# One scaled copy of k moved behind two evictions on VectorE, and a warm-up loop six units shorter

## The chip, the cores and the metric

The kernel runs on one core of a Trainium2 chip. The metric is device time in microseconds (us): the median of three runs of the kernel before is 266.46 us (265.84 to 266.88). The profile is of a single execution of the same program. TensorE (PE), VectorE (DVE), ScalarE (ACT) and GpSimd (POOL) do the work; SyncE (SP) issues most of the transfers.

## The reference

```
q, k, v: (8, 12, 448, 64);  x = attention output, heads side by side: (8, 448, 768)
q_n = q / sqrt(mean(q*q, -1) + 1e-6) * g_q          # the same for k with g_k
attn = softmax(q_n @ k_n.T / sqrt(64));  x = attn @ v
h = relu(x @ w_in);  u, w = h[..., :512], h[..., 512:]      # w_in: 768 x 1024
w_n = (w - mean(w, -1)) / sqrt(var(w, -1) + 1e-6)
gated = u * (w_spatial @ w_n + b_spatial)            # w_spatial: 448 x 448, over the sequence
out = gated @ w_out                                  # 512 x 768, float32
```

## The kernel before

The attention part works in 24 groups. Group G is four heads of one batch (three groups make a batch), so group 15 is the first of batch 5. The steps of a group are short functions named by one letter:

- L loads q or k (second number 0 for q, 1 for k) to a tile `raw`; Q squares it to `sqt`; R sums the squares on DVE (`ss`); I and J turn the sums of q and k to `rs` by Ln and Exp on ACT; N multiplies `raw` by `rs` to the bf16 tile `nrm`, mostly on POOL.
- T is a transposing DMA, issued by SP, from `nrm` to `qT`, or for k to `kr`. Z then multiplies `kr` by a column of gains (`g_col`) to `kT`; it is the scaled copy of the title. Groups 0 to 3 go by matmul transposes (p, P) and copies (k, K) instead.
- S makes scores on PE into two PSUM banks, in 7 units (c = 0 to 6) of a group; E takes the exponential of such a pair on ACT (`et`). s, a and b are the passes over `et` that give the sums of the softmax and the two halves of attention times v; D and d on ACT make the reciprocal sums, X on DVE writes the normalised result to `xt`.

The other part works on one batch at a time, a few steps behind: V and U are the two halves of x times `w_in`; c and u are their ReLU evictions from PSUM; B, M, m and A are the normalisation of the c half; H is the product with `w_spatial`, G the gate, O the product with `w_out`, o its eviction to `os`, t the store. v loads v, and W does the rows left over (384 to 447) of V and O.

The order of all of it is written out by hand: a long string `PLAN` has one word for every step. `S.15.0/23` is step S of group 15, unit 0, into banks 2 and 3; a last part `/v`, `/a` or `/g` names the engine (VectorE, ScalarE, GpSimd). Each engine executes its own words strictly in this order and waits, by semaphores, for what a step reads or overwrites. Because buffers are few (2 tiles `kr`, 4 `kT`, 3 `sqt`, 8 PSUM banks), a late step also holds up whoever writes its buffer next.

One more rule ties DVE and POOL. Steps of either that go through `port` (Q, N, Z from `kr`, A) take turns, so that each waits for the last such step that the other engine has ahead of it in the plan:

```
def port(eng, inst):
    other = on_port.get("g" if eng is dve else "v")
    if other is not None:
        sync_dep(inst, other)
    on_port["v" if eng is dve else "g"] = inst
```

`z.72.18/0` is a warm-up loop on PE in front of the first real matmuls. Its results are not used. The first number counts units of 128 columns, the second says how many matmuls are 512 columns wide (four units each); the rest are 128 wide, so 72.18 is 18 wide matmuls and 66.16 is 16 wide and 2 narrow ones (L269 in the profile). The steps right behind it are the first transposes of group 0 (p.0.0, L469), which read `nrm` from n.0.0 on DVE (L450).

Lines of the profile that come up below: L302 step L, L391 Q, L403 R, L418 and L425 I and J, L442 N, L497 T, L480 Z on DVE, L523 S, L532 E, L558 the passes s, a and b, L577 and L581 D and d, L587 X, L596 c and u on DVE, L603 V, L677 U, L713 O, L372 and L370 o on DVE and on ACT, L323 v.

Of the kernel before, what the change touches and what calls it, by code (L numbers as in the profile page):

```python
# [18 lines left out]

PLAN = """  # L20
setup//v l.1.0/0 l.0.0/1 l.0.1 g.1//a g.0//a l.1.1 L.1.1/2 q.0.0/0/v r.0.0//v L.1.0/3 L.2.1/4 q.1.0/1/g r.1.0//v wb//g
L.2.0/5 i.0//a j.0//a n.0.0//v z.72.18/0 p.0.0/0 q.1.1//a ws//g gA//v q.0.1//a k.0.0/0/a L.3.1/6 gB/7 n.1.0//v p.1.0/6
r.0.1//v L.5.0/7 r.1.1//v L.3.0/8 v.0.2//g i.1//a j.1//a Q.1.1/2/g gC//v k.1.0/0/v z.16.4/1 S.0.1/67 Q.1.0/1/a
S.0.2/01/f n.1.1//v p.1.1/2 L.4.1/0 n.0.1//v p.0.1/3 R.1.1/0/v wo.0//g k.0.1//v E.0.2/0/a R.1.0//v L.4.0/1 k.1.1//a
Q.2.1/0/g R.2.1/1/v z.16.4/4 S.0.5/23/f S.0.4/01 Q.2.0/2/g E.0.1/1/a I.1.0/0/a v.0.1//g J.1.0/0/a S.0.6/45 E.0.6/2/a
# [62 lines left out]
X.10.1//v V.3.2.1/1 v.4.2//g S.13.4/45 G.2.0//v T.15.1/0 E.13.1/a/a Q.19.0/0/a S.13.3/23 E.13.4/g/a E.13.3/3/a  # L88
G.2.1//v W.3/076 S.13.5/45/f t.0.0 S.14.4/23/f V.3.2.2 L.18.0/3 R.16.1//v I.16.0/0/a c.3.3//v O.2.1.0/0 Q.18.1/1/g
V.3.2.0 J.16.0/0/a N.16.0/2/g o.2.3.1/2/v o.2.3.0//v S.13.6/67 o.2.1.0/3/v E.14.4/8/a E.13.5/0/a c.3.2//a B.3.3//v  # L90
S.13.2/23 t.2.3 E.13.6/i/a v.4.0//g Z.15/1/v S.14.1/45 E.14.1/9/a U.3.3.0/0 v.4.1//g U.3.3.2 U.3.3.1 u.3.3//v
O.2.1.1/7 o.2.1.1//v S.13.0/45 s.12.5.1/01 R.18.1/1/v s.12.6.1 E.13.2/5/a E.13.0/d/a s.12.4.1 N.16.1/3/g T.16.1/0
B.3.2//v S.15.0/23 S.14.6/67 E.15.0/6/a R.17.0/2/v s.12.1.1 s.12.2.1 E.14.6/c/a S.15.2/45 s.12.0.1 s.12.3.1 D.12/1/a
D.13/0/a Q.17.1/1/g R.17.1//v T.16.0/0 V.3.0.0/3 V.3.1.2/2 V.3.1.1 V.3.0.1 R.19.0/0/v E.15.2/b/a L.19.1/2 O.2.2.0/1
V.3.0.2 c.3.0//v O.2.0.0/0 I.17.0/0/a V.3.1.0 c.3.1//v Q.18.0/2/g R.18.0//v B.3.1//v J.17.0/0/a N.17.0/1/g b.12.6.1/76
# [687 lines left out]
```

## Time and profile before

| | |
|---|---|
| runs, median (lowest to highest) | 266.46 us (265.84 to 266.88) |
| the profiled execution | 268.54 us |
| its span, first to last instruction | 266.7 us |
| busy: PE, DVE, ACT, POOL | 254.9, 213.3, 216.8, 127.5 us |
| instructions | 9428 |
| granted TensorE clock, mean | 0.985 |

The span is 1.8 us shorter than the time of the same execution; that rest lies around the instructions. The profiled execution took 2.1 us longer than the median of the runs without a profile, so a sum over its rows is made against 268.54 us. An engine's busy time alone says little here, since four engines hand work to each other all the time; what counts is which wait ends last at a given place. In the rows of a timeline, the first number is the start in us from the first instruction, the second how long the row lasted; rows of equal instructions are merged ("x24"), and a bracket tells of idle time ahead of the row and of what ended it. Ends and starts of neighbours on one engine overlap by a few hundredths, because instructions are pipelined.

### The profile page before, as it was taken

To read this page: it belongs to the slowest core of one execution; us is meant where nothing else is said; L and a number is where in the kernel's file an instruction comes from. 1 tells how busy PE (TensorE), PEld (TensorE's weight loads), DVE (VectorE), ACT (ScalarE), POOL (GpSimd) and SP (SyncE) were. 2 spreads that over 40 slices of the span, in tenths; PEclk is the share of its full clock that TensorE was granted. 3 is DMA by queue.
4 is the path that set the end of the run, shared out by engine and by line. 5 is a ranking of instruction groups with operands and counts; after the bars stand their busy time and mean duration, and the time that the engine had idled before them with its cause. 6 is when DMAs were issued, how large, how long until landed. Compare 5 with 4: busy or idle time off the path is not lost.

```text
span 266.7 us, 9428 instructions
## 1 busy us (share of the span) xinstructions
PE 254.9 (96%) x4025; PEld 129.4 (49%) x4041; DVE 213.3 (80%) x368; ACT 216.8 (81%) x357; POOL 127.5 (48%) x109
## 2 busy tenths in 40 slices
PE   7989999999999999999999999999999999999993
PEld 2454435434545456454455454454455555455561
DVE  4899799998698999979799988898983564476861
ACT  1788999999999999997899999997989983332522
POOL 3686246778874789267888577518210000000000
PEclk9995999999999999999999999999999999999999
DMA  6999997999999999999999999999952051031136
GB/s 194 328 306 312 225 258 98 161 232 222 147 233 288 226 240 187 329 204 186 238 240 223 211 248 182 180 196 264 228 115 118 2 209 32 2 124 57 29 158 227
DMA packets 62690, 51.08 MB, mean 192 GB/s; under 512 B 39160, under 2 KB 58808, under 8 KB 62648
## 3 DMA queue, kind: packets, MB, share of 16 engines
q1 hardware_dynamic: 54304, 42.02, 63.4%
q0 software_dynamic: 8192, 8.27, 20.2%
q8 instruction: 31, 0.51, 0.8%
q10 hardware_dynamic: 152, 0.20, 0.2%
q14 instruction: 11, 0.09, 0.1%
HBM read 38.55 MB, written 11.01 MB: 186 GB/s over the span
## 4 chain that ended last, share of the span: by engine, by line
PE 66%; DMA 11%; DVE 8%; ACT 7%; POOL 4%; issue 3%; SPq 0%; POOLq 0%; DVEq 0%
PE ps L558 13%; PE ps L677 11%; PE ps L523 10%; PE ps L713 10%; PE ps L603 9%; PE ps L691 7%; ACT et L532 5%; DMA raw<-in_q_dram 5%; PE ps L637 3%; DMA qT<-nrm 3%; DMA kr<-nrm 3%; POOL nrm L442 3%; DVE xt L587 1%; DVE ss L403 1%; POOL sqt L391 1%
## 5 line engine op out<-in xcount | busy, mean ns | idle before, releaser
L532 ACT ACTIVATE et<-ps 128x896 bf16<-128x896 f32 x168 | 145.3, 923 | 8.1 <-PE ps L523 7.3
L442 POOL TENSOR_TENSOR nrm<-raw,rs 128x896 bf16<-128x896 f32 x32 | 53.7, 1690 | 23.8 <-ACT rs L425 7.3
L391 POOL TENSOR_TENSOR sqt<-raw 128x896 f32<-128x896 f32 (+1 forms) x28 | 46.1, 1650 | 35.4 <-DVE sqt L391 20.1
L523 PE MATMUL ps<-qT,kT 64*32 64x448 bf16 (+1 forms) x1060 | 59.2, 361 | 2.7 <-DMA qT<-nrm 0.6
L403 DVE TENSOR_REDUCE ss<-sqt 128x14 f32<-128x896 f32 x46 | 49.0, 1077 | 1.2 <-POOL sqt L391 1.0
L558 PE MATMUL ps<-et,vt 64*32 64x448 bf16 x1344 | 44.8, 350 | 0.0
L677 PE MATMUL ps<-xt,w_in 128*128 128x448 bf16 x192 | 43.8, 353 | 0.1
L523 PEld LDWEIGHTS <-kT 64*32 64x32 bf16 (+1 forms) x1060 | 21.6, 94 | 33.6 <-issue 21.6
L713 PE MATMUL ps<-w_out,gt 128*128 128x384 bf16 (+1 forms) x196 | 37.5, 323 | 0.1
L603 PE MATMUL ps<-w_in,xt 128*128 128x512 bf16 x128 | 35.6, 380 | 1.0 <-issue 0.3
L587 DVE TENSOR_TENSOR xt<-ps,rc 128x448 bf16<-128x448 f32 x48 | 27.6, 615 | 7.8 <-PE ps L558 6.5
L370 ACT ACTIVATE os<-ps 128x384 f32<-128x384 f32 (+3 forms) x34 | 15.8, 477 | 16.1 <-PE ps L713 12.3
L558 PEld LDWEIGHTS <-vt 64*32 64x32 bf16 x1344 | 22.3, 92 | 12.0 <-issue 3.5
L691 PE MATMUL ps<-w_spT,vn 128*128 128x448 bf16 (+1 forms) x128 | 27.7, 353 | 0.1
L677 PEld LDWEIGHTS <-w_in 128*128 128x128 bf16 x192 | 17.5, 98 | 19.8 <-issue 5.3
L323 POOL DMA_DIRECT2D vt<-in_v_dram x36 | 24.0, 668 | 6.5 <-PE ps L523 6.5
L558 PE MATMUL ps<-et,ones 64*32 64x448 bf16 x672 | 25.9, 353 | 0.4 <-ACT et L532 0.4
L713 PEld LDWEIGHTS <-gt 128*128 128x128 bf16 x196 | 18.3, 98 | 16.0 <-issue 2.8
L372 DVE COPY os<-ps 128x384 f32<-128x384 f32 (+3 forms) x33 | 17.3, 535 | 10.7 <-PE ps L713 6.7
L696 DVE TENSOR_TENSOR gt<-ps,us 128x448 bf16<-128x448 f32 x32 | 19.5, 622 | 6.9 <-PE ps L691 6.1
L652 DVE BATCH_NORM_STATS2 s<-vs 128x6 f32<-128x512 bf16 (+1 forms) x32 | 21.8, 682 | 1.6 <-ACT vs L594 1.4
L603 PEld LDWEIGHTS <-xt 128*128 128x128 bf16 x144 | 12.7, 97 | 16.7 <-issue 5.4
(61 smaller groups left out, 255.8 us busy)
## 6 DMA issues: line engine op xcount, KB each, us to landing
raw<-in_k_dram SPq DMA_DIRECT2D x23, 448.0 KB, 6.1
raw<-in_q_dram SPq DMA_DIRECT2D x23, 448.0 KB, 5.7
out_dram<-os SPq DMA_DIRECT2D x23, 384.0 KB, 3.1
vt<-in_v_dram POOLq DMA_DIRECT2D x24, 112.0 KB, 5.8
vt<-in_v_dram POOLq DMA_DIRECT2D x12, 224.0 KB, 7.4
out_dram<-os SPq DMA_DIRECT2D x9, 192.0 KB, 4.3
w_in<-in_moe_w_in_dram POOLq DMA_DIRECT2D x1, 1536.0 KB, 14.1
w_out<-in_moe_w_out_dram POOLq DMA_DIRECT2D x4, 192.0 KB, 4.5
```

The lines of the kernel that those rows point to most:

```text
L323: pool.dma_start(out=vts[b % 2][64 * halves[0]:64 * halves[0] + 64 * len(halves), g].rearrange("p r c d -> p r (c d)"), in_=src)
L391: port(eng, eng.tensor_tensor(out=t, in0=x, in1=x, op=ALU.mult))
L403: dve.tensor_reduce(out=sss[where["ssl", pair[G]]][:, G - pair[G], i].rearrange("p r c -> p (r c)"), in_=sqt[where.pop(("sq", G, i))].rear ...
L442: port(eng, eng.tensor_tensor(out=nrm[sl[0]].rearrange("p c r d -> p r c d"), in0=raw[where["raw", G, i]].rearrange("p r (c d) -> p r c d" ...
L523: pe.matmul(out=ps[at:at + w, sl[n], 0:S], lhsT=kT[64 * r:64 * r + 64, c, 64 * hh + x:64 * hh + x + w], rhs=qT[64 * r:64 * r + 64, :, 64 * ...
L532: act.activation(out=ets[sl[0]].rearrange("k n (p c) -> k n p c", c=C), in_=ps[:, a:a + 2, 0:S].rearrange("k n (c p) -> k n p c", p=T), fu ...
L558: pe.matmul(out=ps[32 * l:32 * l + 32, where[kind, G][0], 0:S], lhsT=w, rhs=et_of(G, r, c)[at:at + 64], start=(n == 1), stop=(n == C), til ...
L587: dve.tensor_tensor(out=xts[b % 2][:, 2 * g + half, :], in0=ps[:, where.pop(("ab"[half], G))[0], 0:S], in1=rcs[where["rc", G]], op=ALU.mult)
L603: pe.matmul(out=ps[:, bank, :], lhsT=xts[b % 2][:, j, 128 * m:128 * m + 128], rhs=w_in[:, j // 2, j % 2, DH:], start=(n == 1 and j == 2 * ...
L677: pe.matmul(out=ps[:, bank, 0:S], lhsT=w_in[:, j // 2, j % 2, 128 * f:128 * f + 128], rhs=xts[b % 2][:, j, :], start=(n == 1 and j == 2 * ...
L691: pe.matmul(out=ps[:, sl[0], 0:S], lhsT=vns[b % SLOTS["vn"]][rows, m, 128 * f:128 * f + 128], rhs=w_spT[rows, m, :], start=(m == 0), stop= ...
L713: pe.matmul(out=ps[:, sl[0], 0:n], lhsT=gts[b % 2][:, f, 128 * m:128 * m + 128], rhs=w_out[:, f, x:x + n], start=(f == 0), stop=(f == 3))
```

## The change

Z.15 (the scaled copy of k of group 15, on DVE) moves down in the plan, behind u.3.3 and o.2.1.1, which are two evictions of PSUM on the same engine. Seen by the other engines it also moves behind S.14.1, E.14.1, the U.3.3 and O.2.1.1 matmuls and the DMA v.4.1, but these sit on other engines and keep their places there. The warm-up loop loses two wide matmuls and gains two narrow ones.

```
-... n.0.0//v z.72.18/0 p.0.0/0 ...
+... n.0.0//v z.66.16/0 p.0.0/0 ...
-S.13.2/23 t.2.3 E.13.6/i/a v.4.0//g Z.15/1/v S.14.1/45 E.14.1/9/a U.3.3.0/0 v.4.1//g U.3.3.2 U.3.3.1 u.3.3//v
-O.2.1.1/7 o.2.1.1//v S.13.0/45 s.12.5.1/01 R.18.1/1/v ...
+S.13.2/23 t.2.3 E.13.6/i/a v.4.0//g S.14.1/45 E.14.1/9/a U.3.3.0/0 v.4.1//g U.3.3.2 U.3.3.1 u.3.3//v
+O.2.1.1/7 o.2.1.1//v Z.15/1/v S.13.0/45 s.12.5.1/01 R.18.1/1/v ...
```

On VectorE, at 133.85 us of the profile before, the order of instructions changes as follows. L652 and L653 are B.3.3, L480 is Z.15 (reading the tile `kr` and writing the second `kT`), L596 is u.3.3, L372 is o.2.1.1 and L403 is R.18.1.

```order
 L652 BN_STATS s61_151<-vs1_132 64x6 [waits DVE_49]
 L653 BN_AGGR mv1_145<-s61_151 64x2 [waits DVE_49]
+L596 TENSOR_SCALAR us1_136<-ps_63 128x448 [waits PE_49]
+L372 COPY os3_142<-ps_63 128x384 [waits PE_49,Activation_49]
 L480 TENSOR_SCALAR kT1_87<-kr0_84,g2_col_162 128x896 [waits DMAHW6_49,Pool_49]
-L596 TENSOR_SCALAR us1_136<-ps_63 128x448 [waits PE_49]
-L372 COPY os3_142<-ps_63 128x384 [waits PE_49,Activation_49]
 L403 TENSOR_REDUCE ss1_114<-sqt1_74 128x14
 L652 BN_STATS s60_150<-vs1_132 128x6
```

The copy's own waits stay the same: the landing of a DMA (T.15.1) and POOL (its turn behind N.16.0).

On TensorE the order of instructions stays the same. What changes is a wait, at the first weight load of S.15.0 (135.48 us of the profile before), behind the last pass of s.12.4 (L558):

```order
 L558 LDWEIGHTS ones_159
 L558 MATMUL ps_63<-et16_106,ones_159 32x448
-L523 LDWEIGHTS kT1_87 [waits DMAHW5_49]
+L523 LDWEIGHTS kT1_87 [waits DMAHW5_49,DVE_49]
 L523 MATMUL ps_63<-qT3_83,kT1_87 32x448 [waits Activation_49]
 L523 LDWEIGHTS kT1_87
```

The load now waits for DVE itself. Before, the wait of the first pass of s.12.5, a few rows ahead, covered it: that pass writes bank 0, which u.3.3 empties, and u.3.3 stood behind Z.15.

At the start of the program, on TensorE, the end of the warm-up loop changes; the L469 rows are p.0.0:

```order
 L269 MATMUL ps_63<-ident_156 128x512
 L269 LDWEIGHTS ident_156
-L269 MATMUL ps_63<-ident_156 128x512
+L269 MATMUL ps_63<-ident_156 128x128
 L269 LDWEIGHTS ident_156
-L269 MATMUL ps_63<-ident_156 128x512
+L269 MATMUL ps_63<-ident_156 128x128
 L469 LDWEIGHTS nrm00_125 [waits DVE_49]
 L469 MATMUL ps_63<-ident_156,nrm00_125 64x128
```

The instructions of ScalarE, GpSimd and SyncE stand in the same order with the same waits.

More of the change, by code (lines that the diff above doesn't have):

```diff
@@ L21 @@
 setup//v l.1.0/0 l.0.0/1 l.0.1 g.1//a g.0//a l.1.1 L.1.1/2 q.0.0/0/v r.0.0//v L.1.0/3 L.2.1/4 q.1.0/1/g r.1.0//v wb//g
-L.2.0/5 i.0//a j.0//a n.0.0//v z.72.18/0 p.0.0/0 q.1.1//a ws//g gA//v q.0.1//a k.0.0/0/a L.3.1/6 gB/7 n.1.0//v p.1.0/6
+L.2.0/5 i.0//a j.0//a n.0.0//v z.66.16/0 p.0.0/0 q.1.1//a ws//g gA//v q.0.1//a k.0.0/0/a L.3.1/6 gB/7 n.1.0//v p.1.0/6
 r.0.1//v L.5.0/7 r.1.1//v L.3.0/8 v.0.2//g i.1//a j.1//a Q.1.1/2/g gC//v k.1.0/0/v z.16.4/1 S.0.1/67 Q.1.0/1/a
@@ L90 @@
 V.3.2.0 J.16.0/0/a N.16.0/2/g o.2.3.1/2/v o.2.3.0//v S.13.6/67 o.2.1.0/3/v E.14.4/8/a E.13.5/0/a c.3.2//a B.3.3//v
-S.13.2/23 t.2.3 E.13.6/i/a v.4.0//g Z.15/1/v S.14.1/45 E.14.1/9/a U.3.3.0/0 v.4.1//g U.3.3.2 U.3.3.1 u.3.3//v
-O.2.1.1/7 o.2.1.1//v S.13.0/45 s.12.5.1/01 R.18.1/1/v s.12.6.1 E.13.2/5/a E.13.0/d/a s.12.4.1 N.16.1/3/g T.16.1/0
+S.13.2/23 t.2.3 E.13.6/i/a v.4.0//g S.14.1/45 E.14.1/9/a U.3.3.0/0 v.4.1//g U.3.3.2 U.3.3.1 u.3.3//v
+O.2.1.1/7 o.2.1.1//v Z.15/1/v S.13.0/45 s.12.5.1/01 R.18.1/1/v s.12.6.1 E.13.2/5/a E.13.0/d/a s.12.4.1 N.16.1/3/g T.16.1/0
 B.3.2//v S.15.0/23 S.14.6/67 E.15.0/6/a R.17.0/2/v s.12.1.1 s.12.2.1 E.14.6/c/a S.15.2/45 s.12.0.1 s.12.3.1 D.12/1/a
```

## The prediction

> **What bounds the kernel now.** I read the page's busy times and its chain first, then the chain of waits around and behind the moved copy, then the timelines of the four engines around 134 us, and last the start. From the page:
>
> ```profile
> PE 254.9 (96%) x4025; PEld 129.4 (49%) x4041; DVE 213.3 (80%) x368; ACT 216.8 (81%) x357; POOL 127.5 (48%) x109
> PE 66%; DMA 11%; DVE 8%; ACT 7%; POOL 4%; issue 3%; SPq 0%; POOLq 0%; DVEq 0%
> ```
>
> PE has work for 96% of the span and holds two thirds of the chain that ended last. Whether PE also has slack at the place of the change is told by the busy times of stretches (length, then busy time of PE, weight loads, DVE, ACT and POOL):
>
> ```profile
> 135.00:137.00 2.00, 2.00 (x88) 1.22 (x84) 1.92 (x3) 2.00 (x4) 1.48 (x2) 1.00 1.22 253
> 141.00:143.00 2.00, 2.00 (x81) 1.37 (x88) 1.93 (x4) 2.00 (x5) 2.00 (x2) 1.00 0.92 311
> 168.00:266.00 98.00, 93.57 (x1338) 49.34 (x1343) 65.74 (x126) 63.25 (x108) 13.18 (x13) 1.00 0.51 129
> ```
>
> From 135 to 143 us all four are nearly full: nobody has a gap in which to hide a delay. From 168 us PE stays near full while DVE and ACT have a third of their time free. In the chain of waits from 155 us to the end PE is left only once for long:
>
> ```profile
> 159.94 0.02 DVEq L587
> 160.00 2.23 DVE xt L587 x4
> ```
>
> These are X.14 and X.15, which wait for PE's own passes by way of ACT. So what PE loses at 135 to 145 us is not regained by a wait that would have come anyway; it moves the end.
>
> **The moved copy, before.** DVE around it:
>
> ```profile
> 133.18 0.17 DVE L653 BATCH_NORM_AGGREGATE mv<-s 64x2 f32<-64x6 f32 x1
> 133.85 0.62 DVE L480 TENSOR_SCALAR kT<-kr,g_col 128x896 bf16<-128x896 bf16 x1 [0.49 <-DMA kr<-nrm]
> 134.39 0.61 DVE L596 TENSOR_SCALAR us<-ps 128x448 bf16<-128x448 f32 x1
> 135.08 0.56 DVE L372 COPY os<-ps 128x384 f32<-128x384 f32 x1
> 135.55 1.07 DVE L403 TENSOR_REDUCE ss<-sqt 128x14 f32<-128x896 f32 x1
> ```
>
> DVE stands idle for 0.49 us until the transposed k has landed, copies, and goes on with the two evictions. The question is whether these were kept waiting by the copy. Their inputs on PE:
>
> ```profile
> 133.01 1.31 PE L677 MATMUL ps<-xt,w_in 128*128 128x448 bf16 x6
> 134.16 0.81 PE L713 MATMUL ps<-w_out,gt 128*128 128x384 bf16 x4
> 135.10 0.75 PE L558 MATMUL ps<-et,ones 64*32 64x448 bf16 x24
> 135.67 0.56 PE L523 MATMUL ps<-qT,kT 64*32 64x448 bf16 x16
> ```
>
> The matmuls of u.3.3 (L677) end at 133.01 + 1.31 = 134.32, and it began at 134.39. Those of o.2.1.1 (L713) end at 134.16 + 0.81 = 134.97, and it began at 135.08. Both began as soon as PE had delivered, so taking the copy out of their way gains nothing here; the idle time of DVE only moves from the front of the copy to the front of the evictions.
>
> **What the move costs, step by step.** (1) On DVE the copy takes the place at 135.55. Its usual length is in the view of the tile `kr`:
>
> ```profile
> L480 DVE TENSOR_SCALAR kT<-kr,g_col x16: 435/446/621, 52.1 to 195.3; 128x896 bf16<-128x896 bf16 x16
> DMA to landing us min/median/max: 2.9/4.6/8.3
> ```
>
> Its 0.62 us is the longest of 16; I take the median of 0.45, since POOL, which was issuing transfers of v until 134.25 (below), will be idle. It ends at 136.00. The sentence of a page on this: the Trainium skill, "SBUF — State Buffer", on the two physically separate sides, says that VectorE and GpSimd share a pair of ports which the one that starts first holds for its whole instruction, and that descriptors of GpSimd's transfers need it too. By that rule the long copy is such a meeting and 0.45 holds; without it the copy would keep 0.62 and the sum below would be 0.17 us larger.
>
> (2) PE's S.15.0 reads this copy. It began at 135.67 (first of the L523 x16); with the copy done at 136.00 and some 0.1 us to the first matmul it begins at about 136.1: 0.45 us later, and PE executes in order.
>
> (3) POOL takes turns with DVE, so N.16.1 waits for the copy:
>
> ```profile
> 132.88 1.37 POOL L323 DMA_DIRECT2D vt<-in_v_dram  x2
> 134.56 1.69 POOL L442 TENSOR_TENSOR nrm<-raw,rs 128x896 bf16<-128x896 f32 x1 [0.30 <-DVE kT L480]
> 136.76 3.42 POOL L391 TENSOR_TENSOR sqt<-raw 128x896 f32<-128x896 f32 x2 [0.52 <-POOL nrm L442]
> 140.37 3.34 POOL L442 TENSOR_TENSOR nrm<-raw,rs 128x896 bf16<-128x896 f32 x2 [0.19 <-ACT rs L425]
> ```
>
> It began 0.09 us after the copy's end (134.47), so now at 136.09, which is 1.53 us later, and ends at 137.78. Behind it is Q.17.1. Before, that step did not follow at once: it waits for R.18.1, which reads the same `sqt` (135.55 + 1.07 = 136.62, then 136.76). This wait takes up part: Q.17.1 now begins at about 137.74 (neighbours overlap 0.04), 0.98 us later.
>
> (4) From here everything is tight. R.17.1 on DVE reads Q.17.1, and ACT's I.17.0 reads R.17.1:
>
> ```profile
> 138.48 1.09 DVE L403 TENSOR_REDUCE ss<-sqt 128x14 f32<-128x896 f32 x1
> 140.47 0.68 DVE L596 TENSOR_SCALAR vs<-ps 128x512 bf16<-128x512 f32 x1
> 139.66 0.32 ACT L418 ACTIVATE ls<-ss,eps 128x28 f32<-128x28 f32 x1
> 141.04 0.48 ACT L370 ACTIVATE os<-ps 128x384 f32<-128x384 f32 x1
> 143.75 0.46 DVE L480 TENSOR_SCALAR kT<-kr,g_col 128x896 bf16<-128x896 bf16 x1
> ```
>
> Q.17.1 ended at 136.76 + 1.68 (half of 3.42, with the overlap) = 138.44, and R.17.1 began at 138.48; I.17.0 began 0.09 us after R.17.1's end. So c.3.0 (140.47), I.17.0, o.2.0.0 (141.04), N.17.0 (140.37, on `rs`), N.17.1, and Z.16 (143.75, which waits its turn behind N.17.1's end at 143.71) all move by 0.98 us. PE needs three of them at once:
>
> ```profile
> 141.31 0.37 PE L523 MATMUL ps<-qT,kT 64*32 64x448 bf16 x8
> 141.50 0.37 PE L558 MATMUL ps<-et,vt 64*32 64x448 bf16 x8
> 144.45 0.38 PE L523 MATMUL ps<-qT,kT 64*32 64x448 bf16 x8
> ```
>
> S.14.0 (141.31) writes bank 3, emptied by c.3.0 0.15 us earlier; the pass at 141.50 writes bank 0, emptied by o.2.0.0 at 141.52; S.16.1 (144.45) reads Z.16's copy, done at 144.21. With these 0.98 us later PE is 0.98 us late at 142 us and still at 145. That includes the 0.45 us of step (2); the two don't add.
>
> (5) The queues behind: SP issues T.16.1 when N.16.1 is done, 1.53 us later, and T.16.0, L.19.1 and L.20.1 stand behind it.
>
> ```profile
> 136.27 1.26 SPq L497 DMA_TRANSPOSE kr<-nrm  x1
> 125.83 3.19 SPq L497 DMA_TRANSPOSE kr<-nrm  x1
> ```
>
> T.16.1 then goes out at 137.80 and has until Z.16 at 144.73, which is 6.9 us; the median landing takes 4.6. I cost it at nothing; the cover is gone at a landing over 6.9 us (a rival below).
>
> **The warm-up loop.**
>
> ```profile
> 1.69 6.27 PE L269 MATMUL ps<-ident 128*128 128x512 bf16 x18 [1.69 <-POOL ident masks.py:199]
> 8.13 0.58 PE L469 MATMUL ps<-ident,nrm 128*64 128x128 bf16 x7 [0.17 <-DVE nrm L450]
> 4.52 10.33 DMA raw<-in_q_dram
> 19.77 0.88 PE ps L461 x7
> ```
>
> The loop ends at 7.96, and the transposes behind it wait for DVE until 8.13 anyway. Two wide matmuls fewer end it some 0.3 us earlier (1.69 + 6.27 over 18 rows is 0.35 us each; the last ones, at full clock, fewer), and the transposes don't move: zero. If the loop ran late, the first transposes would gain at most 2 x 0.35 = 0.7 us, but the chain there is a transfer of q until 14.85 and reaches PE at 19.77; a gain ahead of it is hidden. A loss is only possible by the clock, below.
>
> **The sum.** +0.98 us from the move, 0 from the loop: 268.54 + 0.98 = 269.5 for an execution with a profile, and the same step on the median of the runs, 266.46 + 0.98 = 267.4. Bounds: 0.45 if only step (2) reaches PE; 1.53 if all of N.16.1's delay does. I take 0.98 because three separate waits of PE have the same value.
>
> **Rivals.** *Absorbed.* Runs without a profile are 2.1 us shorter; if their DVE and POOL have some tenths of slack behind 136 us, only step (2) is left, or a part of it: 266.46 + 0.2 = 266.7. For it: POOL's busy share is 48%. Against it: the rows at 138.48, 141.50 and 143.75 start within 0.1 us of what they wait for.
>
> *Faster.* If the transposed k usually lands later than in this profile, the copy used to hold u.3.3, and with it bank 0 and the passes at 135.10, which now run on. Before, Q.17.1 begins 2.91 us after the copy's start (136.76 - 133.85); now at 137.74 whatever the landing, up to 135.55. They are equal when the copy starts at 134.83, so from a landing 1.0 us later than here the move gains, one for one; at 2 us later the time is 266.46 - 1.0 = 265.4. Against it: this landing took 8.0 us (133.85 - 125.83) already, of a longest 8.3.
>
> *T.16.1 lands late.* At 8.3 us after 137.80 Z.16 begins at 146.1, 2.35 us later than before: 268.8. It decides from 6.9 us. The transposes of this stage show 8.0 and 8.3, but the DMA queues are emptier at 137 than at 126.
>
> *The clock.* The stretches around the fall of the granted clock (ahead of DMA's share):
>
> ```profile
> 6.20:9.62 3.42, 3.25 (x25) 1.83 (x24) 2.79 (x6) 2.33 (x5) 1.97 (x3) 1.00 0.99 324
> 9.62:13.03 3.41, 2.95 (x30) 1.29 (x28) 2.77 (x6) 2.51 (x6) 2.65 (x3) 1.00 1.11 330
> 16.45:19.86 3.41, 2.33 (x53) 1.75 (x50) 3.11 (x5) 2.76 (x6) 3.39 (x5) 1.00 1.09 324
> 19.86:26.69 6.83, 6.75 (x79) 3.47 (x82) 6.28 (x10) 5.76 (x8) 4.39 (x4) 0.50 1.14 314
> ```
>
> The clock fell to half at 19.86, behind the stretch in which PE was busy for 2.33 of 3.41 us. The shorter loop takes some 0.3 us from the first of these, which leaves 2.95, as much as the second had, and no fall came after that one. If it fell there, PE would work at half speed from 9.6 us on, so that the 2.95 us of the second stretch would take twice as long; the chain is on a transfer until 14.85, which covers some of it, so the loss is 0 to 3 us, and at the middle the time is 268.0. The Trainium skill, "TensorE: Matmul & The Clock Gate", part 1, has the rule: an idle window of about 3.4 us halves the clock, a busy one restores it, and the window runs freely, so that its borders differ from run to run. The trace agrees with the halving, and the slow stretch lasts 6.83 us, two such windows; no run here shows what the borders do.
>
> **Chances.** The delay is carried as in the sum: 0.58 (266.9 to 268.0 by its bounds). Absorbed: 0.16. Faster by a later landing: 0.12. T.16.1 late: 0.08. The clock: 0.06. A measurement of this kernel tells about 0.5% from no change, so the limits are 265.13 and 267.79. Slower than that: 0.12 of the first case (its upper end), 0.07 of T.16.1 and the clock's 0.06, together 0.25. Faster: 0.08, of the later landing. The rest, 0.67, is no change that can be told. The range 265.9 to 268.4 leaves out about half of the later landing and of T.16.1, most of the clock's, and some of the first case's edge: under 2 in 10.
>
> **What would show it.** In the profile after: u.3.3 within 0.1 us of its matmuls' end as now; the copy about 1.7 us later against the PE rows around it and 0.45 us long; POOL idle ahead of N.16.1 for some 1.8 us with the copy as its end; DVE idle for about 0.6 us ahead of R.17.1; PE idle some 0.4 us ahead of S.15.0 and again around S.14.0; behind 146 us no new wait. It is wrong if DVE waited long for the landing in ordinary runs, if PE's rows behind 145 us are not late by about 1 us, or if the first 30 us differ.

## The result, and the profile after

The changed kernel took 268.62 us (median of four runs, 268.6 to 268.97), the kernel before 266.57 us (median of four runs, 265.84 to 266.88; three of the four are the runs from which the prediction started): a ratio of 1.0084, 95% interval 1.0062 to 1.0106. Forecast were 267.4 us, at most 268.4. Later comparisons gave other ratios for the same two kernels (below): 1.0002, 1.003 and 1.0016. In these most of the first 2 us is gone. Every ratio leaves out the runs that took over 1.5% longer than the fastest of their kernel in the same comparison; in the comparison with 35 runs of before these are its six longest, whose clock was as full as that of the others.

From the page of the profile after (268.6 us, span 266.8 us): busy times, then the shares of the chain that ended last.

```profile
PE 252.8 (95%) x4041; PEld 127.3 (48%) x4041; DVE 213.2 (80%) x368; ACT 216.6 (81%) x357; POOL 127.5 (48%) x109
PE 70%; DMA 8%; DVE 8%; ACT 5%; POOL 3%; issue 3%; SPq 1%; DVEq 0%; POOLq 0%
```

Nothing there tells the two kernels apart; nor do the spans, 266.7 and 266.8 us. The place of the change does. DVE after:

```profile
132.34 0.17 DVE L653 BATCH_NORM_AGGREGATE mv<-s 64x2 f32<-64x6 f32 x1
133.52 0.62 DVE L596 TENSOR_SCALAR us<-ps 128x448 bf16<-128x448 f32 x1 [1.00 <-PE ps L677]
134.24 0.56 DVE L372 COPY os<-ps 128x384 f32<-128x384 f32 x1
134.72 0.44 DVE L480 TENSOR_SCALAR kT<-kr,g_col 128x896 bf16<-128x896 bf16 x1
135.07 1.08 DVE L403 TENSOR_REDUCE ss<-sqt 128x14 f32<-128x896 f32 x1
138.60 1.09 DVE L403 TENSOR_REDUCE ss<-sqt 128x14 f32<-128x896 f32 x1 [0.66 <-POOL sqt L391]
```

The idle time that stood ahead of the copy (L480) now stands ahead of the first eviction, and waits for PE; the copy lasts 0.44 us; R.17.1 (the last row) has a new wait of 0.66 us for POOL. POOL after:

```profile
135.24 1.69 POOL L442 TENSOR_TENSOR nrm<-raw,rs 128x896 bf16<-128x896 f32 x1 [1.83 <-DVE kT L480]
136.90 3.31 POOL L391 TENSOR_TENSOR sqt<-raw 128x896 f32<-128x896 f32 x2
140.50 3.34 POOL L442 TENSOR_TENSOR nrm<-raw,rs 128x896 bf16<-128x896 f32 x2 [0.29 <-ACT rs L425]
```

N.16.1 (first row) sits idle for 1.83 us until the copy is done, and Q.17.1 follows it at once, where before it had waited 0.52 us for DVE. PE after, at S.15.0 and at S.14.0:

```profile
135.21 0.57 PE L523 MATMUL ps<-qT,kT 64*32 64x448 bf16 x16 [0.20 <-DVE kT L480]
141.33 0.38 PE L523 MATMUL ps<-qT,kT 64*32 64x448 bf16 x8 [0.29 <-DVE vs L596]
```

Before, neither row had a wait. To size the loss I take the stage from the start of R.16.1 on DVE to the first weight load of S.16.1, which reads the next group's scaled copy. In the profile after it is

```profile
127.60 1.08 DVE L403 TENSOR_REDUCE ss<-sqt 128x14 f32<-128x896 f32 x1
144.38 0.31 PEld L523 LDWEIGHTS <-kT 64*32 64x32 bf16 x6
```

16.78 us (16.77 from unrounded times), and before it was 144.25 - 128.44 = 15.81: 0.96 us longer. Outside this stage the two executions differ by more than that, in both directions. The steps can be found in every trace by counting each engine's instructions through the plan; the times below are starts, in us, and a minus says that the changed kernel is ahead.

| step | before | after | difference |
|---|---|---|---|
| S.1.0, first load | 21.93 | 20.47 | -1.46 |
| S.3.0, first load | 36.27 | 33.68 | -2.59 |
| S.4.0 | 48.51 | 47.61 | -0.90 |
| R.16.1 | 128.44 | 127.60 | -0.84 |
| S.16.1 | 144.25 | 144.38 | +0.13 |
| end of the last eviction | 262.67 | 262.74 | +0.07 |

Two things stand ahead of the change. In the profile before the clock fell to half from 19.86 to 26.69 us; after, it did not, and PE needs less time for the same work (the first columns are the stretch's length and PE's busy time, the column ahead of the last two is the clock):

```profile
16.00:33.00 17.00, 15.36 (x262) 8.64 (x258) 14.64 (x20) 15.19 (x23) 9.68 (x10) 0.80 1.10 282
16.00:33.00 17.00, 14.22 (x295) 7.96 (x303) 16.13 (x22) 16.52 (x25) 8.40 (x8) 1.00 1.12 295
```

(first row before, second after). And after, PE stood still at 41 us, in the passes of attention times v, where the profile shows nothing that it waited for:

```profile
42.36 0.38 PE L558 MATMUL ps<-et,vt 64*32 64x448 bf16 x5 [1.35 <-issue]
```

So the profiled execution of before (268.54 us) need not be an ordinary one made longer by the profiler. It can be one draw among executions that spread widely, and the next runs bear this out.

### The profile page after: what moved, and what is told of

It is laid out like the page before. It is cut to its first block, busy times and chain, and to the rows that moved or that the text cites. A ratio compares the mean times of both kernels' runs of the same rounds, so it can differ in the third digit from the quotient of the medians.

```text
span 266.8 us, 9445 instructions
## 1 busy us (share of the span) xinstructions
PE 252.8 (95%) x4041; PEld 127.3 (48%) x4041; DVE 213.2 (80%) x368; ACT 216.6 (81%) x357; POOL 127.5 (48%) x109
## 4 chain that ended last, share of the span: by engine, by line
PE 70%; DMA 8%; DVE 8%; ACT 5%; POOL 3%; issue 3%; SPq 1%; DVEq 0%; POOLq 0%
PE ps L558 14%; PE ps L677 14%; PE ps L523 11%; PE ps L713 11%; PE ps L603 9%; PE ps L691 8%; ACT et L532 4%; DMA raw<-in_q_dram 3%; PE ps L637 3%; DMA vt<-in_v_dram 3%; DVE ss L403 2%; POOL sqt L391 2%; DMA qT<-nrm 1%; POOL nrm L442 1%; DVE xt L587 1%
## 5 line engine op out<-in xcount | busy, mean ns | idle before, releaser
L523 PE MATMUL ps<-qT,kT 64*32 64x448 bf16 (+1 forms) x1060 | 57.9, 356 | 3.2 <-DVE kT L480 1.1
L403 DVE TENSOR_REDUCE ss<-sqt 128x14 f32<-128x896 f32 x46 | 49.0, 1077 | 1.9 <-POOL sqt L391 1.6
L558 PE MATMUL ps<-et,vt 64*32 64x448 bf16 x1344 | 45.2, 350 | 1.5 <-issue 1.3
L603 PE MATMUL ps<-w_in,xt 128*128 128x512 bf16 x144 | 37.5, 380 | 0.2 <-DVE xt L587 0.2
L370 ACT ACTIVATE os<-ps 128x384 f32<-128x384 f32 (+3 forms) x34 | 15.8, 478 | 16.1 <-PE ps L713 12.3
L558 PEld LDWEIGHTS <-vt 64*32 64x32 bf16 x1344 | 21.9, 92 | 14.2 <-issue 5.0
L558 PE MATMUL ps<-et,ones 64*32 64x448 bf16 x672 | 25.5, 350 | 0.4 <-ACT et L532 0.4
L372 DVE COPY os<-ps 128x384 f32<-128x384 f32 (+3 forms) x33 | 17.3, 535 | 10.4 <-PE ps L713 6.4
L652 DVE BATCH_NORM_STATS2 s<-vs 128x6 f32<-128x512 bf16 (+1 forms) x32 | 21.8, 682 | 1.6 <-ACT vs L594 1.4
```

Of the source, the lines that this page charges most:

```text
L403: dve.tensor_reduce(out=sss[where["ssl", pair[G]]][:, G - pair[G], i].rearrange("p r c -> p (r c)"), in_=sqt[where.pop(("sq", G, i))].rear ...
L523: pe.matmul(out=ps[at:at + w, sl[n], 0:S], lhsT=kT[64 * r:64 * r + 64, c, 64 * hh + x:64 * hh + x + w], rhs=qT[64 * r:64 * r + 64, :, 64 * ...
L558: pe.matmul(out=ps[32 * l:32 * l + 32, where[kind, G][0], 0:S], lhsT=w, rhs=et_of(G, r, c)[at:at + 64], start=(n == 1), stop=(n == C), til ...
L603: pe.matmul(out=ps[:, bank, :], lhsT=xts[b % 2][:, j, 128 * m:128 * m + 128], rhs=w_in[:, j // 2, j % 2, DH:], start=(n == 1 and j == 2 * ...
```

## The experiments

The theories: A, the change costs what its stage loses, and the rest of the first difference lies in which executions were drawn; B, all of the 2 us belong to the change, by the loop at the start or by the copy.

**The parts alone, and before once more.**

```
b_again    the kernel before
loop_only  z.72.18/0 -> z.66.16/0
move_only  ... v.4.0//g S.14.1/45 ... o.2.1.1//v Z.15/1/v S.13.0/45 ...      (loop 72.18)
one_evict  ... v.4.0//g S.14.1/45 ... u.3.3//v Z.15/1/v O.2.1.1/7 o.2.1.1//v ... (loop 72.18)
```

> The kernel before, once more, for a profile to compare with. Theory A (the first profile of before was an execution that lost about 2 us at the start to the half clock between 20 and 27 us, and its median belongs to executions without that): this profile has a granted clock of about 0.995, a span near 264.7 us, and it reaches the steps at 130 us about 2 us earlier than the first profile. Theory B (the first profile is the usual one and profiling itself costs 2 us): span near 266.7 us, the half clock at 20 us again, steps at 130 us within 0.3 us of the first profile. Ratio 1.000 in both.

> Before, with the shorter warm-up loop alone (66 units, 16 wide). The prediction's step (loop costs nothing): 266.6 us, ratio 0.999 to 1.001, PE not stalled at 41 us for longer than in before. Rival (the shorter loop shifts the first 40 us against the fetches of instructions and of v, and carries the half of the loss that the copy does not explain): 267.6 us, ratio 1.003 to 1.005, with a wait of PE of about 1.3 us near 41 us that before lacks.

> Before, with the copy Z.15 behind the two evictions alone, the loop as before (72 units). The prediction's sum: 266.6 + 1.0 = 267.6 us, ratio 1.0037; steps from 142 us on 0.98 us later than in before's own execution, of which 0.4 at S.15.0. Rival (in executions with the full clock the move costs all of the 2 us): 268.6 us, ratio 1.0077, steps from 142 us on 2 us later.

> The copy Z.15 behind the first of the two evictions (u.3.3) alone, loop as before. By the prediction's working the copy then begins when o.2.1.1 began, 1.2 us later than before at most, at about the same distance behind PE's U.3.3 (0.7 us): it ends about 0.5 us earlier than behind both, S.15.0 is not late by more than 0.1 us, N.16.1 begins about 1.0 us later than in before, Q.17.1 about 0.45 us later, and the time is 266.6 + 0.45 = 267.05 us, ratio 1.0017. Rival (any place behind an eviction costs the same, because the wait is POOL's turn): the same ratio as the move behind both, 1.0037 or more.

| kernel | median us (lowest to highest) | ratio to before, 95% interval | stage us |
|---|---|---|---|
| before, 35 runs | 267.56 (265.18 to 270.57) | | |
| b_again | 268.24 (266.56 to 269.9) | 1.0012 (0.9982 to 1.0041) | 17.34 |
| loop_only | 267.34 (265.14 to 269.54) | 0.9997 (0.9963 to 1.0031) | 16.30 |
| move_only | 268.52 (267.37 to 271.3) | 1.006 (1.0024 to 1.0096) | 16.77 |
| one_evict | 267.21 (265.83 to 270.74) | 0.9984 (0.995 to 1.0018) | 16.08 |

The loop costs nothing that can be told, as forecast. The move's interval holds the forecast 1.0037, and also the rival's 1.0077; its stage is the same as in the changed kernel, to 0.01 us. Behind one eviction the loss is smaller, as forecast: 0.27 us of stage, where 0.45 was forecast; the ratio shows no loss, and the forecast 1.0017 lies at the edge of its interval. For b_again both expectations missed in part: its clock was 0.996, but its span 266.7 us and not 264.7, and the stage took 1.5 us longer than in the first profile of the same kernel. The rows of DVE, POOL and PE there:

```profile
133.89 0.45 DVE L480 TENSOR_SCALAR kT<-kr,g_col 128x896 bf16<-128x896 bf16 x1 [1.85 <-DMA kr<-nrm]
134.26 0.62 DVE L596 TENSOR_SCALAR us<-ps 128x448 bf16<-128x448 f32 x1
134.43 1.68 POOL L442 TENSOR_TENSOR nrm<-raw,rs 128x896 bf16<-128x896 f32 x1 [1.98 <-DVE kT L480]
134.93 0.76 PE L558 MATMUL ps<-et,ones 64*32 64x448 bf16 x24 [1.27 <-DVE us L596]
```

Here DVE waits 1.85 us for the transposed k, u.3.3 stands behind it, and PE waits 1.27 us for the bank that u.3.3 empties. That is the rival called "faster" in the prediction at work, in the kernel before: the execution reached this place early, and the landing did not come earlier with it.

**Again, on other chips, and SP's order.** The last of these lets SP issue the transposed k of group 15 ahead of its q:

```
-... Q.16.1/1/g T.15.0/3 S.12.3/67 ... G.2.0//v T.15.1/0 E.13.1/a/a
+... Q.16.1/1/g T.15.1/0 T.15.0/3 S.12.3/67 ... G.2.0//v E.13.1/a/a
```

> The changed kernel once more, timed beside before on one chip. Theory A (the change costs what the stage from R.16.1 on DVE to the first load of S.16.1 loses, 0.97 us against an execution of before whose copy is not waiting, and less against one that waits for the landing; the rest of the first difference of 2 us lies in which executions of before were drawn): the stage takes 16.77 us again, and the time is 0.4 to 1.1 us over before, ratio 1.0015 to 1.004. Theory B (the whole 2 us belong to the change): ratio 1.0077.

> The kernel before, a third profile. Theory A: the stage from R.16.1 to S.16.1 lies between 15.8 and 17.3 us, as the landing of the transposed k of group 15 has it; no wait of PE at 41 us for more than 0.5 us if that wait belongs to the change, some such wait if it comes by chance (it was in all three profiles with a moved copy and in none of three without).

> The moved copy alone, a second profile. Theory A: the stage from R.16.1 to S.16.1 takes 16.77 us as in the two profiles so far, whatever the landing does. The wait of PE at 41 us: there again if it belongs to the move, absent if it comes by chance.

> The kernel before with SP's T.15.1 (k) ahead of T.15.0 (q), the copy where it was. If the stage of before varies by the landing of T.15.1, which goes out some 1.2 us earlier here: the copy finds its input, the stage takes 15.8 to 16.1 us, and the time is 0.3 to 0.7 us under before, ratio 0.9975 to 0.999. Rival (the landing is set by how full the DMA queues are, not by when SP issues it): the landing comes no earlier, the stage varies as in before, ratio 1.000.

The changed kernel: 267.85 us (265.91 to 268.6), before 267.75, ratio 1.0002 (0.997 to 1.0034), stage 16.77. This excludes theory B; it lies below A's 1.0015 to 1.004, most of which the interval holds. The stage of move_again is 16.77 too, that of b_third 15.78. The wait at 41 us is 1.21 us in after_again, 0.57 in b_third, and absent in move_again, so it comes by chance and does not belong to the move.

In swap_t the copy no longer waits (no bracket), and the stage is 15.81:

```profile
123.41 1.44 SPq L497 DMA_TRANSPOSE kr<-nrm  x1
132.34 0.56 DVE L480 TENSOR_SCALAR kT<-kr,g_col 128x896 bf16<-128x896 bf16 x1
131.94 1.37 POOL L323 DMA_DIRECT2D vt<-in_v_dram  x2
```

Its ratio is 0.9978 (0.995 to 1.0006), the forecast 0.9975 to 0.999.

**A third time, and POOL's turn.** In `turn`, N.16.1 stands ahead of the copy:

```
-... o.2.1.1//v Z.15/1/v ... s.12.4.1 N.16.1/3/g T.16.1/0
+... o.2.1.1//v N.16.1/3/g Z.15/1/v ... s.12.4.1 T.16.1/0
```

> The changed kernel a third time beside before, on whatever chip comes. The stage from R.16.1 to S.16.1 takes 16.77 us again. Ratio: if the stage says all of the change's effect (16.77 against a mean of 16.31 in four profiles of before, 0.46 us), 1.0017, with an interval that holds 1.0002 and not 1.0084; if there is a second effect that the second timing missed, 1.006 or more.

> The changed kernel with POOL's N.16.1 ahead of the copy in the turns of the two engines, so that N.16.1 does not wait for the copy and the copy waits for N.16.1 instead. By the steps of the prediction: N.16.1 begins right behind v.4.1 (0.3 us ahead of where it stood in before), the copy begins at its end, 0.4 us later than in the changed kernel, S.15.0 is 0.85 us late, R.18.1 0.75 us late, and Q.17.1 now waits for R.18.1 and not for N.16.1: the stage from R.16.1 to S.16.1 takes 15.8 + 0.75 = 16.55 us. If POOL's turn had no part in the loss: 16.77 us or more, since the copy is later still.

> The kernel before, a fourth further look at the stage: between 15.8 and 17.35 us, longer the later the transposed k lands against B.3.3's end on DVE.

> SP's T.15.1 ahead of T.15.0 once more: the copy does not wait for its landing, the stage takes 15.81 us again, ratio 0.9975 to 0.999 beside before. If the first ratio was a draw: 1.000 or above.

after_third: 268.01 us, before 267.63, ratio 1.003 (1.0005 to 1.0055), stage 16.77. The interval holds neither 1.0002 nor 1.0084, where 1.0002 had been expected inside. b_fourth: stage 15.80, and a wait of PE at 41 us of 1.03 us. swap_again: 267.14 us, ratio 0.9997 (0.9972 to 1.0023); its copy did not wait either, but DVE had waited 0.78 us for a store that still read an `os` tile, and the stage took 16.21, not 15.81. That SP's other order is faster is not shown.

`turn` missed its number: the stage took 17.22 us, forecast 16.55.

```profile
133.04 1.68 POOL L442 TENSOR_TENSOR nrm<-raw,rs 128x896 bf16<-128x896 f32 x1 [0.62 <-DMA kr<-nrm]
134.76 0.45 DVE L480 TENSOR_SCALAR kT<-kr,g_col 128x896 bf16<-128x896 bf16 x1 [1.04 <-POOL nrm L442]
135.13 1.08 DVE L403 TENSOR_REDUCE ss<-sqt 128x14 f32<-128x896 f32 x1
136.34 3.42 POOL L391 TENSOR_TENSOR sqt<-raw 128x896 f32<-128x896 f32 x2 [1.61 <-issue]
```

N.16.1 does not begin at the end of v.4.1's issue (132.43): it waits for the DMA of T.15.1, which still reads the `nrm` tile that N.16.1 overwrites. I had not seen this wait behind the other. The rest goes as the steps say: the copy at N.16.1's end, R.18.1 behind it, and Q.17.1 0.13 us after R.18.1's end (135.13 + 1.08 = 136.21), as in before. R.18.1 starts 8.52 us after R.16.1 (135.13 - 126.61) against 7.11 in before (135.55 - 128.44): 1.41 us later, and the stage is 17.22 - 15.81 = 1.41 us longer. By its number alone `turn` falls to the rival (16.77 us or more). But here R.18.1 stands behind the copy and holds Q.17.1, so that it does not separate POOL's turn from DVE's own order, as I had meant it to.

**A larger dose.** The copy one instruction further down, behind R.18.1 (loop 72.18):

```
-... o.2.1.1//v Z.15/1/v S.13.0/45 s.12.5.1/01 R.18.1/1/v ...
+... o.2.1.1//v S.13.0/45 s.12.5.1/01 R.18.1/1/v Z.15/1/v ...
```

> Before, with the copy Z.15 behind u.3.3, o.2.1.1 and also behind R.18.1, loop as before. Theory (the stage's loss is the delay of Q.17.1, which follows N.16.1, which follows the copy): against an undisturbed execution of before the copy begins 1.0 us later than behind the two evictions, N.16.1 and Q.17.1 too, Q.17.1 1.98 us late, stage 15.8 + 1.98 = 17.8 us, and the time 0.97 to 1.98 us over before, ratio 1.004 to 1.007. Rival (the loss comes from S.15.0's own wait or is bounded by slack behind it): stage under 17.4 us.

> The changed kernel, a fourth comparison. If the stage is all of the effect: ratio 1.000 to 1.004. If there is more: 1.006 or above.

> The kernel before, a fifth profile: the stage from R.16.1 to S.16.1 between 15.8 and 17.35 us.

```profile
134.68 0.45 DVE L480 TENSOR_SCALAR kT<-kr,g_col 128x896 bf16<-128x896 bf16 x1
135.18 0.57 PE L523 MATMUL ps<-qT,kT 64*32 64x448 bf16 x16 [1.19 <-DVE kT L480]
135.21 1.69 POOL L442 TENSOR_TENSOR nrm<-raw,rs 128x896 bf16<-128x896 f32 x1 [2.87 <-DVE kT L480]
136.86 3.31 POOL L391 TENSOR_TENSOR sqt<-raw 128x896 f32<-128x896 f32 x2
```

`late`: stage 17.80 us, as forecast; ratio 1.006 (1.0019 to 1.01), inside the forecast. Q.17.1 again starts right at N.16.1's end (135.21 + 1.69, less the overlap). Against an undisturbed execution the stage loses 0.27, 0.96 and 1.99 us as the copy stands behind one, two and three instructions: what Q.17.1 loses, the stage loses. That is theory A's chain, from the copy by N.16.1 to Q.17.1. Five profiles side by side tell it from the rivals (us after the start of R.16.1; for S.15.0 and S.16.1 the first weight load):

| profile | copy starts | S.15.0 | R.18.1 ends | Q.17.1 starts | S.16.1 (the stage) |
|---|---|---|---|---|---|
| before | 5.41 | 7.04 | 8.19 | 8.32 | 15.81 |
| b_again | 7.24 | 8.66 | 9.68 | 9.82 | 17.34 |
| after | 7.11 | 7.61 | 8.55 | 9.30 | 16.77 |
| turn | 8.15 | 8.66 | 9.60 | 9.73 | 17.22 |
| late | 8.14 | 8.64 | 8.22 | 10.32 | 17.80 |

In `turn` and `late` the copy and S.15.0 stand at the same place, and yet the stage differs by 0.58 us, as Q.17.1 does: the loss is not S.15.0's own wait. In `late` R.18.1 ends as early as in before, so only N.16.1, which waits its turn behind the copy, holds Q.17.1. In all 17 profiles, whatever the order, S.16.1 comes 7.47 to 7.52 us behind the start of Q.17.1.

after_fourth: 268.04 us, before 267.36, ratio 1.0016 (0.9987 to 1.0044), stage 16.77. b_fifth took 270.5 us, with a stage of 17.40, 0.05 above what was expected:

```profile
135.45 0.45 DVE L480 TENSOR_SCALAR kT<-kr,g_col 128x896 bf16<-128x896 bf16 x1 [2.39 <-DMA kr<-nrm]
135.99 1.69 POOL L442 TENSOR_TENSOR nrm<-raw,rs 128x896 bf16<-128x896 f32 x1 [2.04 <-DVE kT L480]
136.49 0.76 PE L558 MATMUL ps<-et,ones 64*32 64x448 bf16 x24 [1.50 <-DVE us L596]
```

**All profiles together.** Times in us; "copy waits" is DVE's idle time until the landing.

| copy | profiles | copy waits | stage |
|---|---|---|---|
| where it was | before, b_third, b_fourth | 0.49, 0, 0.5 | 15.81, 15.78, 15.80 |
| where it was | loop_only, b_again, b_fifth | 1.31, 1.85, 2.39 | 16.30, 17.34, 17.40 |
| behind two evictions | after and its three repeats, move_only, move_again | none for the landing | 16.77 in all six |

So the move puts a fixed 16.77 in place of a stage that is 15.8 if the copy is done by the time that PE has delivered to u.3.3, and longer if not: in the three profiles whose copy waited over 1 us, the stage is the copy's start (6.21, 7.24 and 7.30 us after R.16.1) plus 10.1 us. The two orders cost the same where that gives 16.77, with a copy that starts 6.7 us after R.16.1; in the first profile it started at 5.41.

The mean of the six profiles with the copy where it was is 16.41, and the move costs 0.36 us against it; six values this far apart leave that mean uncertain by some 0.8 us (95%). An estimate from more executions: 15 of the 17 profiles have SP's order of before. With the landing of T.15.1 in each, the copy 0.1 us behind it, and the rule above, the stage of the old order would average 16.2 us, and the move costs 0.6.

The times agree: in the three later comparisons the changed kernel's 36 runs average 267.95 us, and 112 later runs of before (without the six that the ratios leave out, and without b_fifth) 267.51 (265.18 to 269.9). The difference of 0.44 has a 95% interval of 0.11 to 0.77 from the spread of the runs (ratio 1.0016, 1.0004 to 1.0029). Against all 119 later runs of before it is 0.30 (-0.04 to 0.64): the times by themselves hardly tell the cost from none, and its size rests on the stage.

## Why the prediction was right or wrong

**What failed was the base of the sum, and a range without the spread.** "The same step on the median of the runs, 266.46 + 0.98 = 267.4": the 266.46 us came from three runs within 1.0 us, and I took it for the kernel's time. The later 112 runs of before lie between 265.18 and 269.9 us and average 267.51, 1.05 us more. With this base the sum would have been 267.51 + 0.98 = 268.5; that it would have met the 268.62 is luck, since the changed kernel's later 36 runs average 267.95. I had the sign of it in hand: the profiled execution took 268.54 us, and I put its 2.1 us down to the profiler ("runs without a profile are 2.1 us shorter"). No such cost shows later: in the ten kernels timed with twelve runs each, the profiled run lies 0.1 us above the median of its twelve on average, above it in five and below it in five. That execution was a draw from the upper part of the spread. The range had no term for this spread at all, and 268.62 fell outside it. This does not explain the first comparison itself, in which before stood at 266.57 and the difference of 2.05 us was twice the step: the stage has 0.96 us of it, and where the rest comes from stays open (below).

**The step itself was right, against that execution.** The working said +0.98 us; the stage gained 0.96. Its parts: the evictions gained nothing (u.3.3 now waits 1.00 us for PE); the copy took 0.44 us, forecast 0.45; N.16.1 waited 1.83 us, forecast some 1.8; measured from R.16.1 it began 1.52 us later than before (forecast 1.53), and Q.17.1 0.98 us later (forecast 0.98); R.17.1 waited 0.66, forecast about 0.6; PE waited at S.15.0 and at S.14.0; against R.16.1, S.14.0 was 0.86 us later than before and S.16.1 0.96, forecast 0.98 for both. The bracket at S.15.0 shows only 0.20 us; counted by PE's passes, those behind S.15.0 stand 0.45 us ahead of before where R.16.1 stood 0.84 ahead, so 0.39 us is lost by 136 us, forecast 0.45.

**As a mean, 0.98 was too much.** The prediction took the landing of its one profile as the usual one, and gave a later landing 0.12, from 1.0 us on. In two of six profiles the copy waited long enough that the stage took longer than the move's 16.77; in a third the stage was half a microsecond longer than undisturbed (16.30). The argument against it, that this landing was already among the longest, looked at the wrong thing: what matters is when k lands against the arrival of DVE and PE, and the two shift against each other. In the first profile SP had issued T.15.1 2.61 us ahead of R.16.1 (125.83 and 128.44), in b_again only 1.87 us ahead (124.78 and 126.65) and in b_fifth 1.00 (127.15 and 128.15). The lead alone does not decide: in b_third it was 1.49 us, and the copy did not wait, since the landing took 6.2 us there, against 7.9 in the first profile and 9.0 in b_again. The point from which the move gains was also off: the prediction had a landing 1.0 us later than in its profile, and it is 1.3 (6.7 less 5.41). The mean loss is 0.4 to 0.6 us by the stages, and it is the mean that a comparison of many runs shows.

**The others.** T.16.1's landing had cover, as costed: Z.16 moved by 0.12 us between the two profiles as N.17.1 did, so it waited for POOL, not for the landing. One argument for it was wrong: the DMA queues were not emptier at 137 than at 126 us, their busy share in the profile before is 0.94 from 125 to 127 us and 1.17 from 136 to 138. The loop cost nothing, as costed. The clock rival did not happen in the four profiles of the changed kernel. "Absorbed" did not happen either: the stage kept its full loss in all six profiles with the moved copy, and the stretch behind it, from S.16.1 to S.20.1, takes 30.6 to 31.5 us in profiles with and without the change; from S.20.1 to the last eviction it is 87.6 to 87.8 us in all 17.

**Open.** Why the eight runs of the first comparison lay so close together, four low and four high, is not shown. A quarter of the later runs of before are as low as its four (266.88 or less), and a quarter of the later runs of the changed kernel as high as its four (268.6 or more), so eight independent draws would hardly fall like that. Three of before's four are those that stand ahead of the prediction, so the eight need not have been drawn side by side. Something that stayed the same within each group is likely, but which thing was not found. move_only's 1.006 is also higher than its stage explains; against all 35 runs of before its mean is 1.06 us higher (1.004), about what the stage gives.

## What to carry to other kernels

Before a prediction adds a step of 1 us to a median of three runs, it should ask how far executions spread: a profile that is 2 us off the median is evidence of spread, and the wait that an edit removes must be judged by how early its engine arrives in other executions, not by one. An in-order engine that waits early for a slow transfer may be the cheaper arrangement: putting the waiter further down made its cost the same in every execution, and made everything behind it, here another engine's turn, pay that cost every time. A sum along one chain of waits can be right to 0.02 us and still miss the measured time, if what it is added to is not the mean.

## What the runs showed of the hardware

The scaled copy takes 0.44 to 0.45 us when POOL is idle or at a wait, and 0.56 to 0.62 us where POOL is issuing transfers of v at the same time: 0.62 in the first profile, 0.60 in b_third, 0.58 in b_fourth, 0.56 in swap_t (its rows of POOL and DVE stand above). In swap_again, where 0.23 us of the issue was left when the copy began, it took 0.46. The Trainium skill, "SBUF — State Buffer", section "SBUF: two separate sides", says that the two share a pair of ports that one holds at a time and that GpSimd needs it to write descriptors. The rows agree with a meeting of that kind, but none of the runs took the issue of v away.

The granted clock fell to half in two of 17 profiles: for 6.83 us from 19.86 in the first, and for 3.41 us from 12.54 in one_evict, each time in the first 20 us. It became full between 4.43 us (loop_only) and 7.57 (late), while the warm-up began at 1.68 or 1.69 in each; this moved the end of the warm-up loop. With the shorter loop the first transposes waited for DVE in every profile (0.55 us in the profile after). With the longer one they did not always: in `late` the loop ran to 8.63 us and p.0.0 began at 8.56, where n.0.0 had been done at 7.55. By S.1.6 nothing of this is left to see (20.53 us in `late`, 20.15 in the profile after). The Trainium skill, "TensorE: Matmul & The Clock Gate", part 1, has windows of 3.4 us that run freely; lengths of 3.41 and 6.83 us and borders that differ from run to run agree with it. The idle window that the prediction cites from the Trainium skill fits less plainly: PE was busy in 2.33 of the 3.41 us ahead of the first fall, and in `turn` in 2.31 of the 3.41 us from 4.60 us on, behind which no fall came.

At one place in the passes of attention times v, some 41 us into the span, PE stands still for between 0 and 1.35 us, with and without the change (none, none, 0.57, 1.03 and 1.26 us in the profiles of before, 1.35, 1.21, 0.21 and none in those of the changed kernel). The profile names no cause. The stretch from S.3.0 to S.4.0, which holds it, takes 12.24 us at its shortest and 13.93 at its longest, and this alone is more than the change. The stretch from S.4.0 to R.16.1, also ahead of the change, spreads as far: 78.98 to 80.63 us in the 15 profiles with SP's order of before.
